# Bucket attention and a GELU feed-forward on one core: the softmax division of batch 0 moves from the probabilities to the product with V

## The chip, the cores and the metric

The kernel runs on one core of one Trainium2 chip. The metric is the device time of one execution in microseconds (us). Three executions of the kernel before took 891.5, 893.44 and 896.03 us, with a median of 893.44. The profile shown here is of one execution of 893.21 us; its span, from the first to the last instruction, is 891.4 us, and 1.8 us lie around it.

Engines are named as the profile names them: PE is TensorE (PEld its weight loads), DVE is VectorE, ACT is ScalarE, POOL is GpSimd, SP is SyncE, which issues most of the transfers.

## The reference

Attention over 4 batches of 8 heads with 768 positions and 64 channels, in which a query sees only the keys of its own hash bucket (6 sign bits of a projection), and then a feed-forward layer 512 → 2048 → 512 with an exact GELU over the 3072 rows:

```python
mask = q_bucket[:, :, :, None] == k_bucket[:, :, None, :]
scores = scale * np.matmul(q, k.transpose(0, 1, 3, 2))
scores = np.where(mask, scores, -1000000000.0)
scores = scores - np.max(scores, axis=-1, keepdims=True)
attn = np.exp(scores)
attn = attn / (np.sum(attn, axis=-1, keepdims=True) + 1e-09)
attn_out = np.matmul(attn, v).astype(np.float32)
...
h = x @ w_in
g = 0.5 * h * (1.0 + erf(h * inv_sqrt2))
return (g @ w_out).astype(np.float32)
```

## The kernel before, in words

**Attention.** The work is cut into units: one head and 128 queries against all 768 keys, 48 units in a batch, 192 in all. A unit (`unit`, L938) computes its scores on PE into a PSUM buffer `s` (there are two), takes their largest per row on DVE (L960), makes a scale and a shift from it in two tiny operations (L965, L438 or L434, buffer `rows`), and takes the exponential on ACT (L974), which also delivers the sum of each row. The exponentials stand in a buffer `p` (or, in a slot that is lent later, in `wraw`). A tiny operation adds 1e-9 to the sum (`safe`, L979) and a reciprocal on DVE (L983) makes the factor r.

Batch 0 then goes the float32 way (`whole_turn`, L1024; the setting `WHOLE` says for which pairs of heads, and it is all four pairs in both passes over batch 0): `divide` multiplies the 128x768 exponentials by r, on ACT, DVE or POOL (POOL in two halves of 384); PE transposes them in six blocks of 128x128, three to a PSUM bank `hp` (L1033); ACT or DVE copies each bank into `pt`. Batches 1 to 3 go another way: r is applied while the exponentials are split into two float16 parts `hl`, which a DMA transposes.

For two heads and a chunk of 256 queries, `values` (L1062) multiplies V by the transposed probabilities on PE into one `hp` bank, the two heads in the two halves of the partitions (L1077 in batch 0, L1086 later). Then `high` on ACT (L1107) writes the upper float16 part of the chunk's input x to the feed-forward, and `low` on DVE (L1114) the rest; both read the PSUM bank, and in batch 0 both multiply by V's scale `s_v`. Batch 0 has 4 pairs of heads and 3 chunks, so 12 such products.

**Feed-forward.** For each chunk of 256 rows there are two groups of eight blocks of the 2048 hidden columns. Each group multiplies x by `Win` (L1302), is taken out of PSUM with a scale by ACT (L1312), goes through GELU on ACT (L1340), is split into two float16 parts `g`, and is multiplied by `Wout` (L1384). The weights come as raw 64-bit numbers, are decoded by DVE (L725 to L735) and split by ACT, DVE and POOL during the first 200 us.

**The order.** All of it is a list of steps with needs, buffers and a sort key. `Plan.order` (L120) runs the list through a model of the engines: whenever an engine is free it takes the ready step with the smallest key, and steps that may go to several engines go to whichever takes them first. The instructions are then issued in the order of the starts that the model found. The keys come from the table `PAR`. Each engine executes its own list strictly in order.

**Blanks.** `add_blank` (L389) adds 64 steps of four products of zeros on PE (L393) which need nothing and have the last key of all, so the plan puts one wherever its PE would have nothing else to do, until the 64 are used. They hold one `hp` bank for their time.

```python
        step = add("PE", 0.22, products, 5000.0, [], takes="hp")
        free(step, [step])
```

Of the kernel before, what the change touches and what calls it, by code (L numbers as in the profile page):

```python
# [10 lines left out]
F32 = mybir.dt.float32  # L11
# [22 lines left out]
BLANKS = 64  # L34
# [3 lines left out]
    VB=67.25, GU_DVE=142.88, GU_Pool=372.81, SH_DVE=-85.93, SH_ACT=493.57, SH_Pool=68.35, SF_DVE=-887.75,  # L38
    SF_ACT=162.31, SF_Pool=108.68, SU=-62.77, NM_DVE=132.71, NM_ACT=-36.16, NM_Pool=115.43, NM_SP=44.22,
    NL_DVE=-21.95, NL_Pool=-504.75, XP_ACT=-123.39, XP_DVE=180.18, NK_DVE=-90.24, NK_ACT=-257.23, NK_Pool=-55.95,  # L40
    Z=-107.86, VS0=65.79, H0=-112.84, HL=-846.73, VS=-934.16, G2=389.39, HQ=129.83, VQ=-373.79, in0=-133.17,
    out0=545.05, in1=-218.36, out1=37.81, in2=194.95, out2=21.39, in3=465.04, out3=52.59, H1=3.14, H2=-183.97,
    H3=-155.9, H4=131.48, H5=-603.75, H6=-1004.23, H7=-195.76, MEV=266.52, MGE=696.78, MSP=15.46, V0=-120.7,
    QK0=-118.82, QK1=-287.83, QK2=-180.25, MX0=-320.05, MX1=-49.19, MX2=-219.29, EX0=-612.78, EX1=-167.36,
    EX2=70.44, NR0=-89.58, NR1=33.83, NR2=-17.38, HI0=-561.14, HI1=248.83, HI2=340.6, LO0=106.64, LO1=-1263.75,
    LO2=-161.71, PV0=99.03, PV1=115.36, PV2=-77.27, TR0=-1005.23, TR1=-480.94, TR2=45.98, V1=105.26, V2=-194.1,
    Sin0=149.2, Sin1=64.71, Sin2=7.41, Sin3=246.53, Sout0=-231.58, Sout1=-272.11, Sout2=-372.59, Sout3=194.04,
    Lin=-157, Pin=341.2, Qin=1120.37, Cin=100.83, Min=-140.12, Lout=-105.73, Pout=458.37, Qout=-2863.3,
    Cout=-238.38, Mout=162.39, G0=-122.8, G1=-209.72, G3=488.78, G4=20.46, G5=-83.65, G6=-236.82, G7=27.83,
    DUP0=78.15, DUP1=-85.93, DUP2=-123.07, LOW0=-97.07, LOW1=-66.78, LOW2=18.58, PRJ0=-51.38, PRJ1=841.88,  # L50
    PRJ2=-212.69, MSK0=-114.42, MSK1=426.71, MSK2=228.3, DI_ACT=138.03, DI_DVE=-27.21, DI_Pool=-60.85,
    WS_ACT=419.32, WS_DVE=65.06, WS_Pool=-21.69, WH_ACT=-803.88, WH_DVE=7.52, WH_Pool=-245.54, WL_ACT=-154.68,
    WL_DVE=-7.58, WL_Pool=72.47, VH_ACT=-163.46, VH_DVE=-112.9, VH_Pool=63.2, RND_ACT=86.42, RND_DVE=222.34,
    RND_Pool=221.18, HI_ACT=230.76, HI_DVE=-182.55, HI_Pool=-59.39, DG_ACT=-153.24, DG_DVE=84.64, DG_Pool=151.66,
    EV_ACT=296.59, EV_DVE=1365.55, EV_Pool=34.42, GH_ACT=-144.99, GH_DVE=2.32, GH_Pool=-76.31, NS0=220.81,
    NS1=-94.09, NS2=63.07,
# [7 lines left out]
class Step:  # L64
    def __init__(self, seq, engine, cost, emit, key, needs, takes, table, port, act):
# [5 lines left out]
        self.takes, self.table, self.port, self.act = takes, table, port, act  # L71
        self.needs = [n for n in needs if n is not None]
        self.slot = None
        self.frees = []
        self.start = self.end = None


class Plan:
# [19 lines left out]
    WINDOW = 3.413  # L98

# [4 lines left out]
    def add(self, engine, cost, emit, key, needs=(), takes=None, table=None, port=False, act=1.0):  # L104
        s = Step(len(self.steps), engine, cost, emit, key, needs, takes, table, port, act)
        self.steps.append(s)
        return s
# [12 lines left out]
    def order(self):  # L120
# [33 lines left out]
        while events:  # L154
# [4 lines left out]
            for e in batch:  # L159
# [11 lines left out]
                for u in users.get(e, ()):  # L171
                    left[u] -= 1
                    for w in u.ways:
                        hop = self.SAME.get(w, 0.05) if w == e.engine else self.HOP[e.engine] + self.INTO.get(w, 0.0)
                        at[u, w] = max(at.get((u, w), 0.0), now + hop)
                        heapq.heappush(events, (at[u, w], -1, None))
                    if not left[u]:
                        enlist(u)
            for engine, pool in ready.items():
                if free_at[engine] > now or not pool:  # L180
                    continue
                best = None
                for s in pool:
# [12 lines left out]
                if best is None:  # L196
                    continue
# [20 lines left out]
                if engine == "PE":  # L218

                    while window < int(now / self.WINDOW):  # L220
                        share = busy.get(window, 0.0) / self.WINDOW
                        warm = share > (0.35 if warm else 0.8)
# [19 lines left out]
                count += 1  # L242
                heapq.heappush(events, (free_at[engine], -1, None))
                heapq.heappush(events, (s.end, s.seq, s))
        assert count == len(self.steps), [
            (list(s.ways), s.key, s.takes) for s in self.steps if s.start is None
        ][:10]
        self.time = max(s.end for s in self.steps)
        return sorted(self.steps, key=lambda s: (s.start, s.seq))
# [3 lines left out]
def tile_bucket_attention_moe(  # L253
# [64 lines left out]
    rows = const.tile([P, NT, 6], F32, tag="rows", name="rows")  # L318
    tiny = const.tile([P, 4 * NSC + 2 * B, 4], F32, tag="tiny", name="tiny")
# [58 lines left out]
    hs = const.tile([P, B * H + 3, 8], F32, tag="hs", name="hs")  # L378
# [10 lines left out]
    def add_blank():  # L389
# [5 lines left out]
        step = add("PE", 0.22, products, 5000.0, [], takes="hp")  # L395
# [50 lines left out]
    def affine_on(name, n, pointer=False, psum=False):  # L446

        more = 0.11 if name in ("MV", "MSK", "RND") else 0.0
        return {
            e: (affine_cost(e, n, pointer) + more, PAR[f"{name}_{e}"]) for e in ("ACT", "DVE", "Pool")  # L450
        }

    def subtract_on(name, n):
        return {e: (subtract_cost(e, n), PAR[f"{name}_{e}"]) for e in ("DVE", "Pool")}
# [1021 lines left out]
```

## Time and profile before

| | |
|---|---|
| median of three executions | 893.44 us |
| profiled execution, its span | 893.21 us, 891.4 us |
| mean granted TensorE clock | 0.996 of full |
| PE instructions | 6893 matmuls |
| units of attention, whole way and float16 way | 48 and 144 |
| exponentials on `p` before 210 us | 49 |

A line of the list of groups reads: kernel line, engine, operation, tile written <- tiles read, shapes, count, then busy time in us and the mean ns of one, then the idle time of the engine just before such instructions and what ended most of it. A line of a stretch gives, for each engine, its busy us and in brackets its number of instructions, then the granted TensorE clock as a part of full speed (1.00 is 2.4 GHz, 0.50 is 1.2 GHz; values between are stretches with both), then DMA. A matmul's time is that from its start to its result, and neighbours overlap; so the time that a series takes is read from the timeline, where instructions in a row are merged, and not from count times mean. L438 is the multiply-and-add on DVE or POOL, L434 the one on ACT, whatever uses them.

### The profile page before, as it was taken

The page shows a single profiled execution, that of the slowest core. Times are in us where ns is not written, and L with a number is a line of the kernel's source. Part 1 is how long each engine was busy: PE and PEld are TensorE (multiplying, and loading weights), DVE is VectorE, ACT ScalarE, POOL GpSimd, SP SyncE. Part 2 cuts the span into 40 slices and gives each one's busy share as a digit, 9 for nine tenths or more (in the row PEclk, how much of TensorE's full clock was granted, in tenths as well). Part 3 has the DMA queues.
Part 4 walks back from the last instruction along what each step waited for, and adds up shares of the span by engine and source line. Part 5 has one row for each costly group of instructions (what it writes and reads, how often), then busy time and mean ns, then how long its engine had stood idle before and what let it go on. Part 6 is the DMA issues. An engine that isn't in the chain of part 4 may idle for free. (4 is left out here: it accounts for less than half of the span.)

```text
span 891.4 us, 18270 instructions
## 1 busy us (share of the span) xinstructions
PE 860.6 (97%) x6893; PEld 574.3 (64%) x6893; DVE 675.9 (76%) x1441; ACT 648.6 (73%) x1090; POOL 419.4 (47%) x551
## 2 busy tenths in 40 slices
PE   8999899989999999999999999999999999999998
PEld 5666557655756657667657657657657667676663
DVE  4998999888997999898999898898887851212122
ACT  3788889998897898898998797887877643232221
POOL 2485759686656566655764666455523300000000
PEclk9999999999999999999999999999999999999999
DMA  9952454215687898778879786957766740000000
GB/s 252 258 174 89 117 151 136 72 46 119 145 174 156 167 205 180 150 152 160 170 159 199 155 183 139 179 102 151 135 107 123 132 96 1 24 2 24 1 24 24
DMA packets 282392, 112.15 MB, mean 126 GB/s; under 512 B 228800, under 2 KB 269888, under 8 KB 282304
## 3 DMA queue, kind: packets, MB, share of 16 engines
q1 hardware_dynamic: 282000, 110.98, 57.6%
q8 instruction: 54, 0.88, 0.4%
q14 instruction: 34, 0.28, 0.1%
q10 hardware_dynamic: 304, 0.00, 0.0%
HBM read 43.13 MB, written 6.29 MB: 55 GB/s over the span
## 5 line engine op out<-in xcount | busy, mean ns | idle before, releaser
L1302 PE MATMUL hp<-x,Win 128*128 128x256 f16 x2304 | 265.5, 272 | 1.6 <-DVE x L1114 1.2
L1384 PE MATMUL hp<-Wout,g 128*128 128x512 f16 x1152 | 261.5, 379 | 0.0
L1302 PEld LDWEIGHTS <-Win 128*128 128x128 f16 x2304 | 224.4, 98 | 39.9 <-issue 4.4
L1384 PEld LDWEIGHTS <-g 128*128 128x128 f16 x1152 | 109.9, 98 | 126.3 <-issue 4.4
L960 DVE TENSOR_REDUCE rows<-s 128x1 f32<-128x768 f32 x192 | 179.2, 948 | 8.3 <-PE s L957 5.2
L974 ACT ACTIVATE p<-s,rows 128x768 f32<-128x768 f32 x142 | 140.2, 988 | 19.9 <-POOL rows L438 7.9
L1312 ACT ACTIVATE h<-hp,ffs 128x512 f32<-128x512 f32 x96 | 65.5, 683 | 98.8 <-PE hp L1302 98.2
L956 PE MATMUL s<-Q 88*128 88x384 f16 x304 | 99.4, 327 | 8.2 <-ACT p L974 5.3
L957 PE MATMUL s<-K 128*128 128x384 f16 x304 | 99.2, 326 | 0.0
L438 DVE TENSOR_SCALAR g<-h,ffs 128x512 f16<-128x512 f32 x30 | 15.2, 507 | 108.1 <-ACT h L1340 77.9
L1086 PE MATMUL hp<-pt,vhl 128*64 128x256 f16 x1296 | 77.1, 274 | 0.5 <-DVE o L1414 0.2
L989 DVE SCALAR_TENSOR_TENSOR hl<-p,rows,hl 128x768 f16<-128x768 f32 x66 | 74.1, 1126 | 3.6 <-POOL hl L438 2.0
L1354 DVE SCALAR_TENSOR_TENSOR g<-h,ffs,g 128x512 f16<-128x512 f32 x96 | 73.4, 787 | 2.7 <-ACT g L434 0.6
L1086 PEld LDWEIGHTS <-vhl 128*64 128x64 f16 x1296 | 68.9, 110 | 10.1 <-issue 9.3
L965 POOL TENSOR_SCALAR rows<-rows,hs 128x1 f32<-128x1 f32 x67 | 46.0, 687 | 61.8 <-DVE rows L960 58.1
L438 POOL TENSOR_SCALAR rows<-rows 128x1 f32<-128x1 f32 x109 | 44.2, 406 | 58.3 <-ACT p L974 35.5
L459 POOL TENSOR_TENSOR K<-raw,Q 64x768 f16<-64x768 f32 x40 | 67.7, 1694 | 3.3
L974 ACT ACTIVATE wraw<-s,rows 128x768 f32<-128x768 f32 x50 | 49.4, 988 | 9.4 <-POOL rows L438 3.9
L438 POOL TENSOR_SCALAR raw<-raw,hs 64x768 f32<-64x768 f32 x41 | 46.7, 1139 | 17.9 <-ACT Q L434 8.6
L957 PEld LDWEIGHTS <-K 128*128 128x128 f16 x304 | 29.8, 98 | 30.6 <-issue 13.9
L438 DVE TENSOR_SCALAR rows<-rows 128x1 f32<-128x1 f32 x163 | 28.3, 180 | 26.8 <-ACT p L974 19.6
L438 POOL TENSOR_SCALAR Q<-sign 24x384 f16<-24x384 f16 (+1 forms) x52 | 32.5, 626 | 33.4 <-ACT sign L674 18.5
(169 smaller groups left out, 1366.5 us busy)
## 6 DMA issues: line engine op xcount, KB each, us to landing
raw<-qk SPq DMA_DIRECT2D x27, 384.0 KB, 3.8
vraw<-v SPq DMA_DIRECT2D x24, 384.0 KB, 4.1
wraw<-w_in SPq DMA_DIRECT2D x16, 512.0 KB, 6.1
wraw<-w_out SPq DMA_DIRECT2D x16, 512.0 KB, 4.1
out<-o SPq DMA_DIRECT2D x11, 512.0 KB, 2.9
K<-Q SPq DMA_DIRECT2D x31, 96.0 KB, 2.4
Q<-Q SPq DMA_DIRECT2D x17, 96.0 KB, 2.7
pt<-hl SPq DMA_TRANSPOSE x97, 4.1
```

What stands on the lines that cost most here:

```text
L438: on.tensor_scalar(out=o, in0=x, scalar1=scale, scalar2=bias, op0=ALU.mult, op1=ALU.add)
L459: on.tensor_tensor(out=o, in0=x, in1=y, op=ALU.subtract)
L956: nc.tensor.matmul(to, aq[kk, qs], ak[kk, n], start=True, stop=False)
L957: nc.tensor.matmul(to, bq[:, qs], bk[:, n], start=False, stop=True)
L960: nc.vector.tensor_reduce(out=nm, in_=both(sp), axis=AX.XY, op=ALU.max, negate=True)
L974: nc.scalar.activation(out=buf(ex).rearrange("p (b k) -> p b k", b=2), in_=both(sp), func=AF.Exp, scale=sc, bias=nb, accum_out=ssum,)
L989: nc.vector.scalar_tensor_tensor(out=buf(hi)[:, 1], in0=buf(ex), scalar=r, in1=buf(hi)[:, 0], op0=ALU.mult, op1=ALU.subtract,)
L1086: nc.tensor.matmul(pv[j * D : (j + 1) * D], buf(vh)[:, tv, kt, j * D : (j + 1) * D], buf(holds[j][0])[:, tp * KT + kt, :nt], start=kt == 0 ...
L1302: nc.tensor.matmul(buf(pair[0])[:, j * ch[1] : (j + 1) * ch[1]], win_hl[:, f0 // WB1, tw, pr, f0 % WB1 : f0 % WB1 + P], x[:, tx, pr, : ch[1]],
L1312: nc.scalar.activation(out=values_of()[:, 2 * fp : 2 * fp + 2, :nt], in_=buf(pair[0])[:, : 2 * nt].rearrange("p (j k) -> p j k", j=2), fun ...
L1354: nc.vector.scalar_tensor_tensor(out=gt[:, 1, s2, :nt], in0=h[:, s2, :nt], scalar=sg, in1=gt[:, 0, s2, :nt], op0=ALU.mult, op1=ALU.subtract,)
L1384: nc.tensor.matmul(buf(banks[u]).rearrange("p (c f) -> p c f", c=NWB), gt[:, tg, f, u * P : (u + 1) * P], wout_hl[:, :, tw, ft], start=ft ...
```

## The change

Four edits.

1. In batch 0 the exponentials are transposed undivided. `unit` writes the row sums of both heads of a pair and a chunk into a tile `sums`. A new function `shares` adds 1e-9 to the four columns of a chunk, takes their reciprocals, and lets PE spread them: for each block of 128 queries and each head, one float32 product of a column, repeated 64 times as weights, with the identity, so that a `hp` bank holds each query's factor in the column of that query, in the 64 partitions of its head. ACT or DVE copies that bank into a buffer of the ring `hl`. In `values`, a DVE operation `weigh` multiplies the product with V by `s_v` and by the factors and writes the result over the factors in that buffer; `upper` (ACT, DVE or POOL) and `lower` (DVE or POOL) make x's two parts from there.
2. There may be up to 128 blanks. The plan puts one only while its own count of PE's recent busy share is at most 0.7, and it ends when all other steps are placed.
3. Some costs and one threshold in the plan's model are changed (the weights' split on POOL is 0.35 to 0.5 us dearer; the model's clock falls at a share of 0.45 instead of 0.35).
4. The table `PAR` has new values throughout, and with them and the above the order of all instructions on all engines is new, their DMAs included.

```diff
-BLANKS = 64
+BLANKS = 128
...
+    FILL = 0.7
+    FALLS = 0.45
...
+                if engine == "PE":
+                    w = int(now / self.WINDOW)
+                    share = busy.get(w, 0.0) / self.WINDOW
+                    share += busy.get(w - 1, 0.0) / self.WINDOW * (w + 1 - now / self.WINDOW)
+                    full = share > self.FILL
...
+                    if s.spare and full:
+                        continue
...
-        step = add("PE", 0.22, products, 5000.0, [], takes="hp")
+        step = add("PE", 0.22, products, 5000.0, [], takes="hp", spare=True)
...
+        if whole:
+            ssum = into
...
+        if whole:
+            return sp, whole_turn(ex, place, cl, t), ex
...
-        if whole:
-            return sp, whole_turn(ex, nr, r, place, cl, t)
...
-        def divide():
-            affine(dg.engine, buf(ex), buf(ex), r, most=512)
...
+    def shares(n, nt, exs, key):
+
+        share = sums[:, n, : nt // P].rearrange("p u j -> p (u j)")
+
+        def sure():
+            affine(sf.engine, share, share, 1.0, 1e-9)
+
+        def norm():
+            nc.vector.reciprocal(out=share, in_=share)
+
+        def spread():
+            for u in range(nt // P):
+                for j in range(2):
+                    nc.tensor.matmul(
+                        buf(rt)[j * D : (j + 1) * D, words(u)],
+                        sums[:, n, u, j : j + 1].broadcast_to([P, D]), ident32, start=True, stop=True,
+                    )
+
+        def copy():
+            affine(rc.engine, wide(rc)[:, :nt], buf(rt)[:, :nt])
...
+            def weigh():
+                nc.vector.scalar_tensor_tensor(
+                    out=wide(share)[:, :nt], in0=buf(parts[0])[:, :nt], scalar=s_v[:, b : b + 1],
+                    in1=wide(share)[:, :nt], op0=ALU.mult, op1=ALU.mult,
+                )
+
+            def upper():
+                if (b, ch) != first_ch:
+                    go_late()
+                affine(hi.engine, buf(xt[b, ch])[:, 0, pr, :nt], wide(share)[:, :nt])
+
+            def lower():
+                x = buf(xt[b, ch])
+                subtract(lo.engine, x[:, 1, pr, :nt], wide(share)[:, :nt], x[:, 0, pr, :nt])
```

## Rows read from the trace of the kernel before

**Rows 1.** The page's first part: busy us, share of the span and number of instructions of each engine over the whole span.

```profile
PE 860.6 (97%) x6893; PEld 574.3 (64%) x6893; DVE 675.9 (76%) x1441; ACT 648.6 (73%) x1090; POOL 419.4 (47%) x551
```

**Rows 2.** Busy time of each engine in five stretches of the span, with the granted clock.

```profile
0.00:25.00 25.00, 21.30 (x235) 15.98 (x236) 13.66 (x36) 10.41 (x19) 6.98 (x26) 0.93 0.94 262
25.00:75.00 50.00, 48.18 (x352) 31.40 (x350) 45.55 (x114) 41.34 (x82) 35.51 (x56) 0.97 0.67 184
75.00:205.00 130.00, 118.29 (x918) 80.12 (x917) 118.98 (x300) 118.28 (x213) 90.87 (x132) 1.00 0.36 102
205.00:715.00 510.00, 500.35 (x4196) 333.71 (x4194) 453.15 (x922) 427.50 (x718) 285.68 (x337) 1.00 0.78 154
715.00:891.40 176.40, 172.51 (x1208) 113.11 (x1202) 44.61 (x73) 51.10 (x61) 0.31 (x1) 1.00 0.09 25
```

**Rows 3.** The timeline of all engines from 886 us to the end.

```profile
885.62 1.89 PE L1384 MATMUL hp<-Wout,g 128*128 128x512 f16 x8
...
887.55 0.69 DVE L1414 TENSOR_TENSOR o<-hp,ffs 128x512 f32<-128x512 f32 x1 [4.49 <-PE hp L1384]
888.27 0.34 SPq L1427 DMA_DIRECT2D out<-o  x1
```

**Rows 4.** The blanks alone (L393), PE and PEld busy in four stretches.

```profile
0.00:25.00 25.00, 13.80 (x174) 12.95 (x175) 0.93 0.94 262
25.00:75.00 50.00, 5.27 (x74) 4.50 (x71) 0.97 0.67 184
75.00:205.00 130.00, 0.83 (x12) 0.76 (x12) 1.00 0.36 102
205.00:715.00 510.00, 0.00 (x0) 0.00 (x0) 1.00 0.78 154
```

**Rows 5.** Who waited for whom from 75 to 205 us: total us, times, longest.

```profile
PEld s L954 <- ACT p L974: 5.7, 9, 1.6
PE s L954 <- ACT p L974: 3.4, 5, 1.5
...
PE hp L1033 <- ACT pt L434: 1.6, 5, 0.4
```

**Rows 6.** ACT's groups of the first 210 us that the change touches, with the copies into `pt`.

```profile
L434 ACT ACTIVATE p<-p,rows 128x768 f32<-128x768 f32 x30 | 27.8, 934 | 5.6 <-DVE rows L983 4.9 <-DVE rows L965 0.4
L434 ACT ACTIVATE pt<-hp 128x384 f32<-128x384 f32 x60 | 27.2, 485 | 3.4 <-PE hp L1033 3.2
...
L434 ACT ACTIVATE rows<-rows 128x1 f32<-128x1 f32 x24 | 5.7, 243 | 2.6 <-DVE rows L965 1.3 <-POOL rows L965 0.9
L1107 ACT ACTIVATE x<-hp,s_v 128x256 f16<-128x256 f32 x12 | 5.6, 467 | 0.8 <-PE hp L1077 0.5
...
L434 ACT ACTIVATE wraw<-wraw,rows 128x768 f32<-128x768 f32 x2 | 1.9, 928 | 0.0
```

**Rows 7.** The same of DVE.

```profile
L438 DVE TENSOR_SCALAR pt<-hp 128x384 f32<-128x384 f32 x36 | 19.5, 548 | 2.9 <-PE hp L1033 2.8
L983 DVE RECIPROCAL rows<-rows 128x1 f32<-128x1 f32 x52 | 8.1, 157 | 2.4 <-POOL rows L438 1.2 <-ACT rows L434 0.9
L438 DVE TENSOR_SCALAR rows<-rows 128x1 f32<-128x1 f32 x48 | 8.0, 176 | 3.5 <-ACT p L974 2.9 <-ACT wraw L974 0.2
L1114 DVE SCALAR_TENSOR_TENSOR x<-hp,s_v,x 128x256 f16<-128x256 f32 x12 | 5.7, 476 | 0.5 <-ACT x L1107 0.5
L438 DVE TENSOR_SCALAR p<-p,rows 128x768 f32<-128x768 f32 x5 | 3.3, 655 | 0.2
```

**Rows 8.** The same of POOL, with its subtractions of 128x256.

```profile
L459 POOL TENSOR_TENSOR Wout<-o,Wout 128x256 f16<-128x256 f32 x24 | 16.4, 713 | 0.1
L438 POOL TENSOR_SCALAR p<-p,rows 128x384 f32<-128x384 f32 x22 | 15.7, 723 | 8.5 <-DVE rows L983 6.2 <-DVE hs L569 1.6 <-DVE tiny L406 0.6
L438 POOL TENSOR_SCALAR rows<-rows 128x1 f32<-128x1 f32 x32 | 14.0, 437 | 14.7 <-ACT p L974 11.1 <-DVE rows L965 1.2 <-DVE hs L569 0.6
```

**Rows 9.** Groups of the whole span whose shapes are nearest to the new operations.

```profile
L1107 ACT ACTIVATE x<-hp 128x256 f16<-128x256 f32 x36 | 13.3, 372 | 10.3 <-PE hp L1086 10.2
...
L459 DVE TENSOR_TENSOR Wout<-o,Wout 128x1024 f16<-128x1024 f32 x2 | 2.5, 1252 | 0.0
...
L438 DVE TENSOR_SCALAR diag<-ident,tiny 128x128 bf16<-128x128 bf16 x3 | 0.7, 245 | 0.0
```

**Rows 10.** PE's timeline from 126 us: start, time of the whole run, number of instructions.

```profile
127.63 1.48 PE L1033 MATMUL hp<-ident,p 128*128 128x128 f32 x12
...
131.17 2.81 PE L1077 MATMUL hp<-pt,vhl 128*64 128x256 f32 x24
...
136.67 1.12 PE L748 MATMUL hp<-Wout 128*64 128x64 bf16 x32
```

**Rows 11.** The weight loads of the products with V (L1077) and of the transposes before 210 us.

```profile
L1033 PEld LDWEIGHTS hp<-ident,p 128*128 128x128 f32 x276 | 31.1, 142 | 16.3 <-issue 4.4 <-ACT pt L434 2.0 <-ACT p L434 1.9
...
L1077 PEld LDWEIGHTS hp<-pt,vhl 128*64 128x64 f32 x192 | 13.3, 137 | 10.2 <-DVE pt L438 1.6 <-ACT pt L434 1.3 <-DVE rows L983 0.5
```

**Rows 12.** PE's timeline from 62 us, around the lower clock.

```profile
65.54 0.70 PE L668 MATMUL hp<-rest,hash 128*32 128x384 f16 x7 [1.24 <-DMA rest<-x]
66.17 1.54 PE L1033 MATMUL hp<-ident,p 128*128 128x128 f32 x6
67.51 2.26 PE L954 MATMUL s<-K,Q 76*128 76x384 f32 x4
...
73.33 1.46 PE L954 MATMUL s<-K,Q 76*128 76x384 f32 x4
```

**Rows 13.** Busy times and granted clock in the stretch that holds the lower clock.

```profile
66.00:70.00 4.00, 4.00 (x20) 2.84 (x18) 1.76 (x3) 3.25 (x7) 4.00 (x7) 0.61 0.47 146
```

**Rows 14.** PE's waits in the whole span.

```profile
PE s L956 <- ACT p L974: 5.3, 13, 1.3
...
PE s L956 <- ACT wraw L974: 2.2, 2, 1.5
```

**Rows 15.** PE's timeline from 20 us, the longest run of blanks.

```profile
22.02 3.30 PE L393 MATMUL hp<-blank 128*128 128x128 bf16 x56
```

**Rows 16.** The instructions of batch 0's products with V: count, duration in ns (least, median, most), start of the first and of the last.

```profile
L1077 PE MATMUL hp<-pt,vhl x192: 379/379/430, 104.1 to 207.4; 128*64 128x256 f32 x192
...
L1077 PE MATMUL hp<-pt,v_first x96: 379/379/431, 39.6 to 86.7; 128*64 128x256 f32 x96
```

More of the change, by code (lines that the diff above doesn't have):

```diff
@@ L64, with __init__ @@
 class Step:
-    def __init__(self, seq, engine, cost, emit, key, needs, takes, table, port, act):
+    def __init__(self, seq, engine, cost, emit, key, needs, takes, table, port, act, spare=False):
         many = isinstance(engine, dict)
@@ L153, in order @@
         count, serial = 0, -1
-        while events:
+        total, again = sum(not s.spare for s in self.steps), 0.0
+        while events and count < total:
             now, _, ended = heapq.heappop(events)
@@ L196, in order @@
                 if best is None:
+                    if full and again <= now:
+                        again = now + 0.3
+                        heapq.heappush(events, (again, -1, None))
                     continue
@@ L241, in order @@
                         heapq.heappush(events, (port_at, -1, None))
-                count += 1
+                count += not s.spare
                 heapq.heappush(events, (free_at[engine], -1, None))
                 heapq.heappush(events, (s.end, s.seq, s))
-        assert count == len(self.steps), [
+        assert count == total, [
             (list(s.ways), s.key, s.takes) for s in self.steps if s.start is None
         ][:10]
-        self.time = max(s.end for s in self.steps)
-        return sorted(self.steps, key=lambda s: (s.start, s.seq))
+        done = [s for s in self.steps if s.start is not None]
+        self.time = max(s.end for s in done)
+        return sorted(done, key=lambda s: (s.start, s.seq))
 @with_exitstack
@@ L936, in head_plain, with unit @@
         return masks, None
-    def unit(t, i, qs, cl, whole, made, place, back):
+    def unit(t, i, qs, cl, whole, made, place, back, into):
         st = rows[:, t % NT]
         nm, sc, nb, ssum, si, r = (st[:, k : k + 1] for k in range(6))
+        if whole:
+            ssum = into
         def both(step):
@@ L1046, in whole_turn @@
             step.append(
[L1047 removed]
+                add("PE", 0.12 * (k1 - k0), lambda k0=k0, k1=k1, step=step: product(k0, k1, step), t + PAR[f"LO{cl}"], [ex], takes="hp")
             )
@@ L1060, in whole_turn, with wide, values @@
         return copies
-    def values(b, pr, ch, whole, vhl, turns, holds, key):
+    def wide(step):
+        return buf(step).rearrange("p t k -> p (t k)").bitcast(F32)
+    def shares(n, nt, exs, key):
[13 more added lines that the diff above has]
+            affine(rc.engine, wide(rc)[:, :nt], buf(rt)[:, :nt])
+        on = {"DVE": (0.09, PAR["SF_DVE"]), "ACT": (0.23, PAR["SF_ACT"]), "Pool": (0.3, PAR["SF_Pool"])}
+        sf = add(on, 0, sure, key + PAR["RN"], exs)
+        nr = add("DVE", 0.08, norm, key + PAR["RN"], [sf])
+        rt = add("PE", 0.24 * nt / P, spread, key + PAR["RT"], [nr], takes="hp", table="half")
+        rc = add(
+            {e: (c, PAR[f"RC_{e}"]) for e, c in (("ACT", 0.31), ("DVE", 0.34))}, 0, copy, key + PAR["RT"], [rt], takes="hl"
+        )
+        free(rt, [rc])
+        return rc
+    def values(b, pr, ch, whole, vhl, turns, holds, key, share):
         vh, vl = vhl
@@ L1213, in tile_bucket_attention_moe @@
                 if pos % 2:
+                    share = shares(pr * NTH + ch[0] // TC, ch[1], exs[ch], t + PAR[f"PV{cl}"]) if whole else None
                     mms.append(
```

114 lines of the change are left out of this document (56 added, 58 removed).

## The prediction

> **What bounds the kernel now.** I read the page's first part, then the stretches, then the end of the timeline, then the waits. PE is busy 97% of the span [rows 1], and the end is PE's: the last product runs until DVE's drain at 887.55 and its store [rows 3]. So the time is the sum of PE's work plus whatever time PE idles or spends on blanks before, and I look for where that is. In 205 to 715 us PE is busy 500.35 of 510 us, 98.1%, with no blank; from 715 on it only streams [rows 2, 4]. The waste is early. In 0 to 25 us 13.8 us of PE's 21.3 are blanks, while the first loads and hashes come in; the change removes no load and no hash from that. In 25 to 205 us, 180 us, PE is busy 48.18 + 118.29 = 166.5 us, of which 5.27 + 0.83 = 6.1 are blanks [rows 2, 4]; so 19.6 us of this stretch bring nothing. What it waits for there is mostly a score buffer that ACT's exponential has not yet freed [rows 5], and ACT is busy 41.3 + 118.3 = 159.6 us of the 180, DVE 45.6 + 119.0 = 164.5, POOL 126.4 [rows 2]. In 75 to 205 us both ACT and DVE stand at 91%: this stretch is bound by the pair. Batch 0's float32 products with V start from 39.6 to 207.4 us [rows 16], so the work that is changed lies there.
>
> **What the change takes away.** 48 divisions of 128x768: 30 + 2 on ACT (27.8 + 1.9 = 29.7 us), 5 on DVE (3.3), 11 on POOL in 22 halves (15.7) [rows 6 to 8]. Of 48 additions of 1e-9 and 48 reciprocals, 12 each remain. The reciprocals save DVE 36 x 0.157 = 5.7 us [rows 7]. The additions are among 24 + 48 + 32 = 104 tiny operations on ACT, DVE and POOL; taking out 36 in these shares saves 8 x 0.243 = 2.0, 17 x 0.176 = 2.9 and 11 x 0.437 = 4.8 us [rows 6 to 8]. The old `high` and `low` of x go: 5.6 us on ACT, 5.7 on DVE [rows 6, 7]. In sum ACT 37.3, DVE 17.6, POOL 20.5: 75.4 us.
>
> **What it adds beside PE.** Twelve times four operations of 128x256. The copy of the factors is nearest to the unscaled read of PSUM, 0.372 us on ACT [rows 9]. `weigh` has the shape of the old `low`, 0.476 us [rows 7]. `upper` lies between 0.245 (a quarter-size multiply on DVE [rows 9]) and 0.723 (128x384 on POOL [rows 8]); I take 0.37, ACT's. `lower` lies between a quarter of the 1.252 us of 128x1024 on DVE, 0.31 [rows 9], and POOL's 0.713 [rows 8]; I take 0.42, nearer to DVE's. That makes 12 x 1.64 = 20 us, with ends 12 x 1.40 = 17 and 12 x 2.28 = 27. The net relief is 55 us, with ends 48 and 58, and on ACT and DVE alone 54.9 - 20 = 35 us when POOL takes none. Copies into `pt` may go to either (60 and 36 of them, 0.485 and 0.548 us [rows 6, 7]), so a relief of ACT reaches DVE too: ten copies moved give DVE 5.5 us.
>
> **What it adds on PE.** 48 float32 products with 128 columns, two heads side by side. A product with V is 12 of 256 columns, and its 24 records take 2.81 us [rows 10], so a side-by-side pair of 256 columns takes 0.47 us and one of 128 columns half, 0.234. 24 pairs make 5.6 us. From below: if 96 short records go as the 64-column products of the weights do, 1.12 / 32 = 0.035 us each [rows 10], 3.4 us. From above: as the transposes do, 1.48 / 12 = 0.123 us each [rows 10], 11.8 us. I take 5.6, from the row of the same kind and dtype.
>
> What the Trainium skill says on the loads speaks against this ("TensorE: Matmul & The Clock Gate", Part 3: Packing small matmuls): a weight load overlaps running products only if it goes to other rows of the array, and both heads' factors use all 128 rows. By it each of 96 loads would stand open; the trace disagrees, for 24 such loads of 0.137 us [rows 11] would alone be 3.3 us and the whole product took 2.81 [rows 10].
>
> **From both to the time.** In 25 to 205 us ACT and DVE carry 324 of 360 us, 90%. With 35 less, at the same density, the stretch would need 289 / 0.90 / 2 = 161 us: 19 less. But PE must do its share as well: 166.5 - 6.1 + 5.6 = 166.0 us, and at the density of the later stretch, 98.1%, that takes 169.2 us. So PE becomes the bound of this stretch, and the gain stops at 10.8 us (13 with the lower price of the spreading, 4.5 with the higher). I take 9: not all of the first heads' stretch can reach the later density, since float32 heads arrive singly. After 205 us nothing of the work changes, and each us won there is won at the end. 893.2 - 9 = 884.2 for this execution, and with the median 0.2 above it 884.4.
>
> **What I cost at nothing.** The new chain (exponentials, addition, reciprocal, spreading, copy, `weigh`, `upper`, `lower`) delays x by some 1.5 us against the old pair. It hides behind the other units' scores and transposes; without that cover it is 12 x 1.5 = 18 us, but only PE's products with `Win` wait for x, and for the first chunk they come long after. The spreading waits for DVE's reciprocal with transposes and scores queued behind it on PE; a transpose no longer waits for a reciprocal and a division, so this queue has gained more slack than it loses. The factors' buffer comes from a ring that batch 0 doesn't use. More blanks: PE is charged only where the plan saw it idle; a run of 56 products takes 3.30 us [rows 15], 0.059 each, so 64 more steps of four cost at most 15 us, if each stood in front of ready work, and nothing if none does; I take nothing, since the plan gives them the last key. They can win back the lower clock at 66 to 70 us (0.61 [rows 13], after a wait of 1.24 us): there four products took 2.26 instead of 1.46 us and six transposes 1.54 against half of 1.48, so 1.6 us [rows 10, 12]. The dearer weight splits and the threshold change only the plan. The new order moves every DMA on SP's queue and every step on POOL's; DMA is 36% busy in 75 to 205 us [rows 2], so I give that nothing, within bounds of -5 to +15 us that stand for the order as a whole: from below half of the 9.65 us that PE idles in 205 to 715, from above twice the idle share there less what the early stretch gives.
>
> **The rivals.**
> - *The relief isn't passed on.* The early units are paced by a chain (scores, largest, exponential, freed buffer) and not by load. For it: PE's waits are for two score buffers [rows 5]. Against it: that exponential is late because ACT is at 91%. Then the spreading takes idle time and the time stays: 892, from 889 to 896.
> - *The order loses in the full stretch* (slower). In 205 to 715 us ACT is 84% and DVE 89% busy, and PE's few waits there are for freed score buffers, 5.3 + 2.2 us in the whole span [rows 14]. If the new order starts each of the 140 later units' exponentials so late that PE waits 0.13 us more, that is 18 us, and 893 - 9 + 18 = 902 (897 to 910). It decides from 9 / 140 = 0.064 us a unit on. Against it: nothing there has more work than before.
> - *The order gains there too.* Half of the 9.65 us of idle time goes, and the early gain is near its upper end: 893 - 13 - 4 = 876 (870 to 879).
> - *The weight loads stand open.* 96 x 0.137 = 13.2 us more on PE: 166.5 - 6.1 + 18.8 = 179.2, or 182.7 at 98.1%, so 896. It is the rule of the Trainium skill named above; [rows 10, 11] speak against it.
>
> **How the numbers follow.** A gain of 4.5 to 14 us, 884.4: 0.48 (its own range 879 to 889). Not passed on: 0.21. Lost in the full stretch: 0.17. Gains twice: 0.09. Open loads: 0.05. 0.5% is 4.5 us, about what a measurement of this kernel can tell from no change: under 889 is faster, over 898 slower. Faster: 0.47 + 0.09 + 0.03 = 0.59; within: 0.01 + 0.17 + 0.04 = 0.22; slower: 0.17 + 0.01 + 0.01 = 0.19. The range 873 to 900 leaves out the far half of the slower case and a third of the best.
>
> **What would show it.** Right: in the first 210 us ACT has some 33 us less to do, no group `p<-p,rows` of 128x768 float32 is left, 96 records of 64 columns stand on PE and take about 5.6 us, the last batch-0 product with V (now starting at 207.4 us [rows 16]) comes some 9 us earlier relative to the feed-forward work done, and PE's idle time from 205 to 715 us stays near 10 us. Wrong: ACT is relieved and PE's waits for score buffers remain; or PE's idle time after 205 us has grown by more than 9 us; or a spreading takes over 0.6 us.

## The result: slower by half a percent, and the profile after

The changed kernel takes 898.34 us (median of 20 executions, 892.61 to 901.91) beside 893.58 us of the kernel before (20 executions, 889.18 to 896.03): a ratio of 1.0052, 95% interval 1.0035 to 1.007. The forecast was 884.4, a ratio of about 0.99. The time lies inside the range, but on the wrong side of 1. By the medians the miss is 13.9 us; the experiments below give 8.1 of them to TensorE's clock and 5.9 to a relief that brought little.

The profiled execution happened to be the fastest of the 20 (892.61 us, granted clock 0.994). An unchanged copy run again (`ctl_after`) took 899.88 us, and its profiled execution, 899.19 us with a span of 897.4, lies near the median; I read that one. Its page's first part, beside [rows 1]:

```profile
PE 872.1 (97%) x6869; PEld 581.7 (65%) x6869; DVE 681.9 (76%) x1387; ACT 615.1 (69%) x1064; POOL 407.7 (45%) x507
```

Over the whole span ACT lost 33.5 us of work and POOL 11.7. DVE, which was to lose 17.6 us less its share of the new work, gained 6.0, and PE gained 11.5. The same five stretches as in [rows 2]; the columns are PE, PEld, DVE, ACT and POOL busy, then the granted clock:

```profile
0.00:25.00 25.00, 21.59 (x121) 11.60 (x122) 13.78 (x37) 11.57 (x21) 6.70 (x22) 0.64 0.94 248
25.00:75.00 50.00, 48.06 (x287) 30.09 (x286) 41.78 (x87) 28.69 (x63) 21.33 (x33) 0.84 0.58 175
75.00:205.00 130.00, 122.72 (x1011) 86.42 (x1010) 115.09 (x264) 106.60 (x205) 80.19 (x107) 0.96 0.38 108
205.00:715.00 510.00, 500.99 (x4206) 336.25 (x4205) 460.96 (x921) 413.58 (x707) 295.75 (x342) 1.00 0.77 152
```

Two things are to be seen. The full stretch from 205 us on is as it was: PE idles 9.0 us there against 9.65. And the clock column has fallen, 0.64 and 0.84 where it was 0.93 and 0.97. Cut more finely:

```profile
0.00:7.00 7.00, 3.59 (x38) 3.41 (x42) 0.93 (x8) 0.00 (x0) 2.59 (x16) 1.00 0.66 152
7.00:40.00 33.00, 32.28 (x164) 16.83 (x157) 23.78 (x48) 17.78 (x33) 8.09 (x14) 0.50 1.03 294
...
93.00:106.00 13.00, 12.01 (x39) 8.20 (x40) 7.60 (x16) 6.96 (x16) 6.36 (x7) 0.61 0.33 94
```

From 7 to 40 us, and for most of the time from 93 to 106 us, PE runs at 0.50, its level of 1.2 GHz. The kernel before had 2.4 GHz but for some 3 us between 11 and 15 us and a part of the 4 us of [rows 13]. It too fell over a wait of 2.08 us; but there 36 blanks followed, 0.106 us each instead of the 0.059 of [rows 15], and behind them the hash products take 0.51 us again and eight score records 2.85 us:

```profile
11.00 0.19 PE L560 MATMUL hp<-tops,twin 128*128 128x1 bf16 x2 [2.08 <-DVE tops L603]
11.05 3.80 PE L393 MATMUL hp<-blank 128*128 128x128 bf16 x36
14.78 0.51 PE L907 MATMUL hp<-Q,hash 64*32 64x384 f32 x1
...
18.46 2.85 PE L954 MATMUL s<-K,Q 76*128 76x384 f32 x8
```

PE's timeline of `ctl_after` (start, length of the run, number of instructions, and the wait ahead of it) shows what that means:

```profile
6.68 0.19 PE L531 MATMUL hp<-offs,shift 128*128 128x1 bf16 x2 [2.43 <-DVE offs L527]
6.80 0.51 PE L923 MATMUL hp<-Q,hash 64*32 64x384 f32 x1
...
9.33 0.85 PE L923 MATMUL hp<-Q,hash 64*32 64x384 f32 x1
...
10.77 2.93 PE L972 MATMUL s<-K,Q 76*128 76x384 f32 x4
...
36.28 3.59 PE L408 MATMUL hp<-blank 128*128 128x128 bf16 x32
...
90.41 0.50 PE L1047 MATMUL hp<-ident,p 128*128 128x128 f32 x3
93.94 1.14 PE L1047 MATMUL hp<-ident,p 128*128 128x128 f32 x6 [3.03 <-DVE tiny L786]
...
97.76 2.77 PE L972 MATMUL s<-K,Q 76*128 76x384 f32 x4
```

Four records of a score step take 2.77 to 2.93 us instead of the 1.46 of [rows 12], a hash product 0.85 instead of 0.51. Each fall follows a wait, one of 2.43 us that ends at 6.68 us and one of 3.03 us that ends at 93.94 us. The blanks alone, to be laid beside [rows 4]:

```profile
0.00:25.00 25.00, 5.35 (x50) 5.09 (x51) 0.64 0.94 248
25.00:75.00 50.00, 5.91 (x56) 5.13 (x54) 0.84 0.58 175
```

The kernel before had 174 blank products in its first 25 us, the changed one has 50. `BLANKS` was doubled, but steps that the new rule (only while PE's recent share is under `FILL`) never finds a place for are not issued: of 128 steps, 34 are left with 136 products, against 64 with 256.

In `ctl_after` the groups of the whole span that answer to [rows 6 to 9] and to the spreading are

```profile
L453 DVE TENSOR_SCALAR pt<-hp 128x384 f32<-128x384 f32 x28 | 15.2, 549 | 1.2 <-PE hp L1047 1.2
L1167 DVE SCALAR_TENSOR_TENSOR hl<-hp,s_v,hl 128x256 f32<-128x256 f32 x12 | 5.8, 482 | 1.9 <-PE hp L1124 1.7
L475 DVE TENSOR_TENSOR Wout<-o,Wout 128x1024 f16<-128x1024 f32 x4 | 5.5, 1371 | 0.1
L475 DVE TENSOR_TENSOR Win<-o,Win 128x1024 f16<-128x1024 f32 x2 | 3.3, 1632 | 0.0
...
L475 POOL TENSOR_TENSOR Wout<-o,Wout 128x256 f16<-128x256 f32 x16 | 11.2, 730 | 0.9 <-ACT Wout L449 0.8
...
L449 ACT ACTIVATE pt<-hp 128x384 f32<-128x384 f32 x68 | 31.2, 490 | 21.7 <-PE hp L1047 21.0
...
L1091 PE MATMUL hp<-ident,sums 128*64 128x128 f32 x96 | 7.8, 283 | 0.7 <-ACT pt L449 0.4 <-DVE rows L983 0.3
```

No group `p<-p,rows` of 128x768 float32 is left. Eight copies into `pt` went from DVE to ACT. Four weight differences went the other way, from POOL to DVE: DVE now does six in 8.8 us where it did two in 2.5 [rows 9], and POOL issues 16 quarters for `Wout` where it issued 24 [rows 8], and 24 for `Win` where it issued 32.

### The profile page after: what moved, and what is told of

Its sections match the earlier page's. It is cut to its first block, busy times and chain, and to the rows that moved or that the text cites. A ratio compares the mean times of both kernels' runs of the same rounds, so it can differ in the third digit from the quotient of the medians.

```text
span 890.8 us, 18120 instructions
## 1 busy us (share of the span) xinstructions
PE 865.2 (97%) x6869; PEld 577.6 (65%) x6869; DVE 681.3 (76%) x1387; ACT 615.3 (69%) x1064; POOL 411.9 (46%) x507
## 4 chain that ended last, share of the span: by engine, by line
PE 56%; DVE 18%; ACT 9%; DMA 9%; issue 4%; POOL 4%; SPq 0%; ACTq 0%; POOLq 0%; DVEq 0%
PE hp L1445 19%; PE hp L1363 18%; PE hp L1133 6%; DVE rows L978 4%; PE s L972 3%; PE s L974 3%; PE s L975 3%; DMA pt<-hl 3%; DVE hl L1007 3%; ACT p L992 2%; PE hp L1124 2%; DMA vraw<-v 2%; DVE g L1415 2%; DMA pt<-wraw 2%; PE hp L1047 1%
## 5 line engine op out<-in xcount | busy, mean ns | idle before, releaser
L992 ACT ACTIVATE p<-s,rows 128x768 f32<-128x768 f32 x144 | 142.3, 989 | 27.3 <-DVE hl L1007 8.5
L453 DVE TENSOR_SCALAR g<-h,ffs 128x512 f16<-128x512 f32 x24 | 12.4, 516 | 109.6 <-ACT h L1401 78.9
L1007 DVE SCALAR_TENSOR_TENSOR hl<-p,rows,hl 128x768 f16<-128x768 f32 x66 | 70.7, 1073 | 8.0 <-POOL hl L453 5.4
L983 POOL TENSOR_SCALAR rows<-rows,hs 128x1 f32<-128x1 f32 x58 | 37.3, 644 | 58.8 <-DVE rows L978 53.5
L475 POOL TENSOR_TENSOR K<-raw,Q 64x768 f16<-64x768 f32 x37 | 61.9, 1674 | 3.1
L992 ACT ACTIVATE wraw<-s,rows 128x768 f32<-128x768 f32 x48 | 47.4, 987 | 9.9 <-POOL rows L453 5.4
L453 POOL TENSOR_SCALAR hl<-p,rows 128x768 f16<-128x768 f32 x29 | 33.9, 1168 | 33.0 <-DMA pt<-hl 16.6
L972 PE MATMUL s<-K,Q 76*128 76x384 f32 x112 | 47.7, 560 | 1.3 <-ACT p L992 1.0
L453 POOL TENSOR_SCALAR raw<-raw,hs 64x768 f32<-64x768 f32 x39 | 43.3, 1110 | 9.4 <-ACT Q L449 6.0
```

The source lines that it names most:

```text
L453: on.tensor_scalar(out=o, in0=x, scalar1=scale, scalar2=bias, op0=ALU.mult, op1=ALU.add)
L972: nc.tensor.matmul(to, q[:, qs], k[:, n], start=True, stop=True)
L992: nc.scalar.activation(out=buf(ex).rearrange("p (b k) -> p b k", b=2), in_=both(sp), func=AF.Exp, scale=sc, bias=nb, accum_out=ssum,)
L1007: nc.vector.scalar_tensor_tensor(out=buf(hi)[:, 1], in0=buf(ex), scalar=r, in1=buf(hi)[:, 0], op0=ALU.mult, op1=ALU.subtract,)
```

## The experiments

A new plan moves every step, so all runs keep the order of one of the two kernels and edit only what is issued. Each is compared with the kernel before, timed beside it on the same chip. CLOCK is the theory that the lost blanks and the lower clock are the loss.

**The same kernel again**, unchanged.

> The changed kernel once more, unaltered, for a second profile. Theory CLOCK (the changed kernel emits 34 blanks instead of 64, 44 instead of 174 of their products in the first 25 us, and TensorE therefore runs at 1.2 GHz in stretches that differ from execution to execution): 896 to 900 us, with a profile in which other or more stretches than 88 to 98 us stand at the lower clock, and the hash products of the first 24 us again take 0.84 us instead of 0.5. Theory ORDER (the new order of the instructions loses, whatever the clock): the same time, but the lost time appears as waits of PE with the clock at full speed.

Measured: 899.88 us (895.0 to 902.9, 8 executions) beside 892.53, ratio 1.007 (1.0038 to 1.0102). The result stands.

**Fewer blanks in the old order.** The blank steps 11 to 43 of the kernel before are issued empty:

```diff
-        add_blank()
+        add_blank(0 if 11 <= n < 44 else 4)
```

> The kernel before with its order kept; of its blanks in the first 25 us only the first 11 emit products (44, as in the changed kernel). CLOCK: PE stays at 1.2 GHz until past 20 us and the time rises by 4 to 8 us, to 898 to 902. LOADS: no change within 1.5 us.

Measured: 900.8 us (897.28 to 905.48), ratio 1.0084 (1.0055 to 1.0113). PE's timeline in its profile:

```profile
17.57 5.49 PE L954 MATMUL s<-K,Q 76*128 76x384 f32 x8
22.99 0.85 PE L907 MATMUL hp<-Q,hash 64*32 64x384 f32 x1
```

The kernel before took 2.85 us for eight such score records. So the blanks that the change no longer issues are worth 8 us in the old order, with nothing else changed. That is CLOCK, as expected, and more than the whole loss; LOADS falls. The 8 us are not the first 25 us alone: this profile has a second fall, 0.65 from 96 to 106 us and 0.77 from 106 to 120 us, where the kernel before has 1.00.

**Only a warm start.** In the changed kernel the first eight blank steps have six products; in the profile of this run the wait that ends at 6.6 us is 1.14 us long, instead of 2.43.

```diff
-        add_blank()
+        add_blank(6 if n < 8 else 4)
```

> The changed kernel with its order kept; only the first eight blanks have 6 products instead of 4 each, so that they fill the 2.03 us in which PE waits for its first input at 4.6 to 6.6 us. CLOCK: PE is at 2.4 GHz from about 7 us on, the hash products and the first scores take half of what they took, and since PE is busy without a pause there, the time falls by 6 to 8 us, to 890 to 892. A rival, LOADS (the first 25 us are paced by the loads, the DMA engines being busy throughout, so the clock there is free): no change within 1.5 us.

Measured: 899.92 us, ratio 1.0077 (1.0048 to 1.0105): missed. The hash products ran in 0.51 us until 14.2 us; then, after float32 work with waits of 0.63 and 0.66 us, the clock fell all the same and stayed down until 39 us. A warm start doesn't hold by itself.

**Relief alone, in the old order.** The kernel before, leaving out batch 0's additions, reciprocals and divisions; the factor 1/32 in the copies stands for them.

```diff
-            affine(dg.engine, buf(ex), buf(ex), r, most=512)
+            pass
```

> The kernel before with its order kept, without batch 0's 48 divisions, additions and reciprocals: that part of the softmax is left out (the copies into pt multiply by 1/32 to keep the sums in range). This gives the relief of ACT, DVE and POOL that the prediction priced, without the spreading and without a new order. Theory RELIEF (the early stretch is bound by ACT and DVE): 5 to 12 us less, 881 to 888. Rival NOT PASSED ON (PE and chains bind it): within 2 us of before.

Measured: 889.91 us, ratio 0.9956 (0.9929 to 0.9983), 2.6 us less at the median; missed by both expectations, between them. ACT from 75 to 205 us fell from 118.28 to 97.64 us and PE still waited for score buffers:

```profile
PE s L954 <- ACT p L974: 2.5, 5, 0.9
PE hp L560 <- DVE pt L438: 1.4, 1, 1.4
PE hp L1079 <- DVE pt L438: 1.2, 1, 1.2
```

Taking 20 us from ACT took 0.9 us from the 3.4 of that wait [rows 5].

**The clock held in the new order.** Blank products are issued ahead of chosen hash, score and transposing steps of the first 40 us, into the PSUM bank that the step overwrites anyway, and during the wait at 84 to 91 us into unused columns of the bank before:

```diff
+            warm("project", buf(pp)[:, :P])
...
+            if nth["product"] == 34:
+                for k in range(40):
+                    nc.tensor.matmul(turned[0][:, 3 * P :], blank, blank, start=True, stop=True)
```

> The changed kernel with its order as it is and 132 more blank products of 128 columns on TensorE: 48, 40 and 28 of them as a prefix in the PSUM bank of a hash, score or transposing step of the first 40 us, 16 in the first eight blank steps (6 products instead of 4), and 40 into the unused columns of a bank during the wait of 2.6 us at 84 us (172 in sum). Nothing of the result changes. CLOCK (the loss is TensorE at 1.2 GHz early on): hash products last 0.48 to 0.51 us throughout the first 45 us, the granted clock stays near 1.00 from 75 to 110 us, and the time falls by 5 to 12 us against the changed kernel, to 886 to 893, ratio to the kernel before 0.993 to 1.000. ORDER or SPREADING (the loss lies elsewhere): the clock is repaired and the time stays at 896 to 900.

> As after_warm, without the 40 products in the wait at 84 us: only the first 40 us are filled. CLOCK: the hash products of the first 45 us at 0.48 to 0.51 us, the lower clock again for some 10 us after the wait at 84 to 91 us, and the time between after_warm and the changed kernel, 2 to 5 us above after_warm. If the second stretch of lower clock costs nothing (TensorE isn't the bound there), the two times agree within 1 us.

The counts in the first text are off: it was 68, 36 and 28 products as a prefix, 16 at the start and 40 in the wait, 188 in sum. Measured: `after_warm` 891.24 us (889.19 to 900.37), ratio 0.9981 (0.9946 to 1.0017). Seven of its ten executions had a granted clock of 0.999 or more and took 889.19 to 891.63 us; the other three, at 0.991 and 0.992, took 895.11 to 900.37. `after_warm_a`, without the 40, took 899.39 us, ratio 1.0038 (0.9998 to 1.0079), 8 us above `after_warm` where 2 to 5 were expected: missed. So the 40 products in the one wait are worth 8 us at the median. The first 40 us must hold too: the profiled execution of `after_warm`, one of the slow three with 900.37 us, fell behind a wait of 1.28 us that ends at 26.07 us, stood at 0.54 from 25 to 40 us, and kept 1.00 from 60 us on. In the profile of `after_warm_a` the first 40 us held (no hash product over 0.51 us) and PE stood at 0.50 from 90 to 96 us. So in these runs either fall alone costs about as much as both; why they don't add up was not shown. The next run puts 32 more blanks at the first place:

```diff
+            n_blank[0] += 1
-            for k in range(4):
+            for k in range(EXTRA["blank"].get(n_blank[0], count)):
```

> after_warm with 32 more blank products in four of the changed kernel's own blank steps at 24 to 27 us (16, 16, 8 and 8 instead of 4 each), where the profiled execution of after_warm fell to the lower clock behind a wait of 1.3 us. Nothing of the result changes. CLOCK: the executions stay at a granted clock of 1.00 nearly all, so their spread shrinks to some 889 to 893 and the median is 890 to 892, 7 to 9 us under the changed kernel and 2 to 4 under the kernel before. If the fall at 25 us has another cause than that wait, a third of the executions is still at 895 to 900.

Measured: 890.26 us (888.71 to 892.34, 12 executions, all at 0.999 or 1.000), ratio 0.9957 (0.9931 to 0.9984). Its stretches:

```profile
0.00:25.00 25.00, 22.38 (x257) 17.05 (x258) 13.97 (x37) 11.87 (x22) 6.75 (x23) 1.00 0.95 245
25.00:75.00 50.00, 48.19 (x368) 31.54 (x366) 45.90 (x96) 31.99 (x71) 21.76 (x34) 1.00 0.63 193
75.00:205.00 130.00, 124.58 (x1087) 88.80 (x1086) 118.77 (x279) 111.79 (x210) 87.94 (x113) 1.00 0.36 104
```

and the wait filled:

```profile
86.17 0.49 PE L1074 MATMUL hp<-ident,p 128*128 128x128 f32 x3
86.50 2.40 PE L1070 MATMUL hp<-blank 128*128 128x128 bf16 x40
88.73 0.82 PE L1074 MATMUL hp<-ident,p 128*128 128x128 f32 x6
```

CLOCK holds: with the order untouched and 220 more products of zeros, the changed kernel is 8 us faster than it was, and the spread of its executions shrinks from 9 us to 3.6. In its profile no hash product of the first 45 us takes more than 0.62 us.

**The old order at the same clock.**

```diff
+            warm("total", buf(pm)[:, :P])
             for k in range(n):
                 nc.tensor.matmul(buf(pm)[:, k : k + 1], twin[:, k], top, start=True, stop=True)
```

> The kernel before with its order as it is and 116 blank products where its own profile and that of before_nodiv fell to the lower clock: 36 and 16 ahead of two scale steps at 11 and 99 us, 16 and 12 ahead of two hash steps at 64 and 97 us, 12 ahead of a score step at 99.5 us, 12 and 12 ahead of two transposing steps at 66 and 97.5 us. Nothing of the result changes. It puts the two orders beside each other at the same clock. If the change's relief is worth something beside the clock, this stays 4 us or more above after_warm2, at 893 to 895. If the clock is all that told the two kernels apart and the relief and the spreading cancel, it comes to 889 to 892, level with after_warm2 within 2 us.

Measured: 894.02 us, ratio 0.9997 (0.997 to 1.0025). Level with before, and no proof that the change is worth 4 us: its 116 blanks stood partly ahead of ready work. Without them, 11 of the 110 executions of the kernel before that were timed beside these runs had a clock of 0.998 or more by themselves; they took 889.87 to 892.46 us, median 890.85. That is a rough mark, for these executions are picked by a column that can read too high early on (see the last section). By it the change at a held clock gives 0.6 us (890.26), no more than nothing, and the relief alone gave 4 (`before_nodiv`: four executions at 0.998 or more, median 886.7).

**The price of the spreading.** Its products twice in the changed kernel, and none (two blanks in the place of eight) with the clock held:

```diff
-            for u in range(nt // P):
+            for u in 2 * [*range(nt // P)]:
```

> The changed kernel with each of its 96 spreading products issued twice (the second to the same place with the same value), 0.6 us more on TensorE for each of the 12 steps, 7.1 us in sum. If TensorE is the bound of the early stretch, the time grows by 5 to 8 us, to 904 to 907, and the spreading of the change itself is paid in full. If it stands in TensorE's waits (the relief isn't passed on and there is idle time), it grows by less than 3 us.

```diff
-                for j in range(2):
...
+                nc.tensor.matmul(buf(rt)[:, words(u)], blank, blank, start=True, stop=True)
```

> after_warm2 with the spreading left out: in each of its 12 steps two blank products of 128 columns stand for the eight products with the sums, so batch 0's rows of x become zero; all else is as it was. That takes 0.59 - 0.12 = 0.47 us from TensorE in each step, 5.6 us in sum. If TensorE sets the pace of the early stretch once its clock is held, the time falls by 4 to 6 us, to 884 to 886. If the spreading stands in TensorE's waits, it falls by less than 2 us.

Measured: doubled 901.61 us, ratio 1.0073 (1.0036 to 1.0111) where `ctl_after` has 1.007, so 0.3 us more by the ratios and 1.7 by the medians, for 7.1 us of PE; left out 889.98 us beside the 890.26 of `after_warm2`, ratios 0.9953 and 0.9957, for 5.6 us less. The spreading stands in PE's waits. The stretches without it, to be laid beside those of `after_warm2`:

```profile
25.00:75.00 50.00, 47.23 (x353) 31.27 (x350) 46.25 (x98) 31.95 (x71) 21.93 (x34) 1.00 0.62 192
75.00:205.00 130.00, 121.19 (x1035) 86.06 (x1034) 117.53 (x279) 112.22 (x211) 88.45 (x113) 1.00 0.36 104
```

PE's busy time fell by 4.4 us and the others' moved by less than 1 us: idle time took its place. PE doesn't set the pace here.

**The division put back in the new order.**

```diff
+                affine(on, buf(ex), buf(ex), 1.0, most=512)
             for k in range(k0, k1):
```

> The changed kernel with a multiplication by 1.0 of 128x768 float32 put back in front of each of the 48 pairs of transposes (32 on ACT, 11 on POOL, 5 on DVE, as the divisions were), in the new order. Nothing of the result changes. If the relief of the change is passed on in the new order, the time grows by 8 to 13 us; if it isn't, by less than 4 us; the kernel before without its divisions gained only 3 to 4 us in its own order.

Measured: 934.92 us, ratio 1.0466, far above either expectation. In its first 240 us PE waited 35.5 us for the multiplied `p` (21.9 on ACT's, 11.0 on POOL's, 2.6 on DVE's): the new plan puts transposes right behind the exponential, and the division now stands between them. This prices a late input in a tight order, not the relief, and I draw nothing else from it.

**Which engine sets the pace, then?** Still with the clock held:

```diff
-                    box[2].engine, dst[:, 1], buf(box[0]).rearrange("p (c f) -> p c f", c=n), dst[:, 0],
+                    "Pool", dst[:, 1], buf(box[0]).rearrange("p (c f) -> p c f", c=n), dst[:, 0],
```

> after_warm2 with the six weight differences that stand on DVE (6 of 16; 5.5 + 3.2 = 8.7 us) issued on POOL instead, at the same place of the order, as 24 quarters of some 0.73 us. Nothing of the result changes. If DVE paces the early stretch, because the change took nothing from it (178.2 us of its work in the first 205 us before, 178.6 in after_warm2), the time falls by 3 to 8 us, to 882 to 887. If DVE isn't what paces it, or what waits for POOL is late instead, it stays at 889 to 892 or above.

```diff
+                for _ in range(2 if box[2].engine == "DVE" else 1):
```

> after_warm2 with the same six weight differences issued twice on DVE (the same result written again), 8.7 us more on DVE. If DVE paces the early stretch, the time grows by 6 to 9 us, to 896 to 899. If DVE has room there, it grows by less than 3 us.

```diff
+                for _ in range(2 if box[1].engine == "ACT" else 1):
```

> after_warm2 with the ten weight copies on ACT (5.3 + 5.1 = 10.4 us) issued twice, 10.4 us more on ACT, which has 10 to 15 us more idle time in the early stretch than before the change. If DVE alone paces the stretch, the time grows by less than 3 us. If ACT does (the pair of ACT and DVE, as the prediction has it), it grows by 5 us or more.

Measured: 898.36, 905.61 and 906.27 us, beside 893.07; ratios 1.0049 (1.0017 to 1.0081), 1.0123 and 1.0129. All three are slower, the one with less work on DVE too. Part is the clock again; PE's timeline of `dve_less`:

```profile
119.55 1.56 PE L994 MATMUL s<-K,Q 76*128 76x384 f32 x4 [1.80 <-ACT p L1014]
120.94 0.22 PE L509 MATMUL hp<-diag,ones 128*128 128x128 bf16 x1
121.00 1.25 PE L1074 MATMUL hp<-ident,p 128*128 128x128 f32 x6
122.05 2.77 PE L994 MATMUL s<-K,Q 76*128 76x384 f32 x4
```

A wait of 0.4 us in `after_warm2` is 1.80 us here, and a new fall follows it, at a place where no blanks were put. In all three profiles the clock column reads 0.92 from 75 to 205 us, where `after_warm2` has 1.00, so a part of each growth is the clock and not the moved work. Where the column reads 0.998 or more, five executions of `dve_less` took 895.0 us at the median, 4.7 above `after_warm2`, and the only one of `dve_more` 901.89, 11.6 above; `act_more` has none. `dve_less` settles less than it was meant to: the differences took 8.7 us on DVE and take some 15 us on POOL, and PE's wait for POOL's `diag`, 0.6 us in `after_warm2`, is now its longest single wait between 25 and 205 us:

```profile
PE hp L509 <- POOL diag L472: 2.6, 1, 2.6
```

So it doesn't tell whether DVE paces the stretch; that DVE alone does is spoken against by `act_more`, which grew as much as `dve_more`. As far as these runs go, work added to DVE is paid in full (one execution), work added to ACT at least in part, and work taken from PE, or handed from DVE to POOL, isn't given back.

**A version that beats both.** `after_warm2` with 48 of its blanks taken out again:

```diff
-    "project": {1: 16, 2: 12, 3: 16, 4: 12, 6: 12},
-    "scores": {0: 8, 1: 12, 2: 8, 3: 8},
-    "product": {0: 16, 2: 12},
+    "project": {1: 16, 2: 8, 3: 12, 4: 8},
+    "scores": {0: 8, 1: 8},
+    "product": {0: 12, 2: 12},
```

> after_warm2 with 48 fewer added blank products: none ahead of the two score steps at 28 and 30 us and of the hash step at 31 us, which stood behind other blanks in front of ready work, and 4 fewer in each of five other places. Nothing of the result changes. If the blanks that are left hold the clock, the time falls by up to 48 x 0.06 = 2.9 us, to 887.5 to 890; if they don't, a part of the executions is at 895 to 900.

Measured: 889.05 us (885.07 to 891.56), ratio 0.9937 (0.9911 to 0.9963): 0.6% under the kernel before and 1% under the changed one. That doesn't take a clock held throughout: its profiled execution, 888.53 us, stood at 0.50 from 22 to 28 us, until 32 blanks had run.

## Why the prediction was wrong, step by step

**The step that failed first** is "More blanks: PE is charged only where the plan saw it idle ... I take nothing", with its sequel that more blanks "can win back the lower clock". I read the doubled count and not the rule beside it. The rule leaves fewer blanks, not more, and the clock was worth not 1.6 us on the good side but 8 on the bad one: `before_fewblanks` (8.3 us more) shows it without the change, `after_warm2` (8.1 us less) undoes it within the change. The sum started from a kernel whose 13.8 us of early blanks I had put down as waste [rows 4]; they were what kept the float32 work of the first 40 us at 2.4 GHz.

**The second** is "From both to the time". It took 35 us from ACT and DVE between 25 and 205 us and turned them into time at an equal density. Neither came out. Of the 35 us, `after_warm2` shows 15.8 on ACT (159.6 [rows 2] to 143.8) and none on DVE (164.5 to 164.7). The terms for DVE were right one by one (no divisions, fewer reciprocals, 5.8 us of `weigh` beside 5.7 forecast), but "the dearer weight splits ... change only the plan" was taken at nothing, and it moved 6.3 us of differences to DVE; with the weights' other steps DVE got 8 us and ACT 4 that POOL had done. And the density was no bound: `before_nodiv` took 25.2 us from ACT and 3.2 from DVE in that stretch without any of the change's costs, and 2.6 us came of it, 4 by the executions with a held clock. In the forecast PE idled 3.2 us of what was left of the stretch from 25 to 205 us and did no blanks; in `after_warm2` it idles 7.2 of the 180 us and does 11 us of blanks, those of the plan and the added ones. With 7.1 us of spreading that is more than the 19.6 us which I had counted as free.

**The spreading** was forecast at 5.6 us and measures 12 x 0.59 = 7.1 on PE (from the start of a step's eight records to the next step, 0.59 instead of 0.47); inside its bounds of 3.4 and 11.8, and worth nothing in the time. A step's own run reads 0.61 to 0.66 us, over the 0.6 us that I had named as a sign of being wrong; that mark stood too near to tell anything. The rival of the open weight loads is refuted: eight records with loads of 0.136 us take 0.66 us, less than eight loads in a row.

**The rivals.** "The order loses in the full stretch" had the right sign and the wrong place: 9.0 us of idle time there. That the time lies in the range at all is owed to this rival, so it is luck. "The relief isn't passed on" is what is left at a held clock, though not for its reason, since PE's waits for float32 score buffers between 25 and 205 us did shrink, from 3.6 us to 1.3 in `ctl_after` and 2.0 in `after_warm2`. Of the marks that I named, the missing group and the idle time after 205 us came as forecast. The relief of ACT in the first 210 us did not: some 33 us were named, and it is 20.7 in `ctl_after` (172.6 to 151.9) and 12.0 in `after_warm2`; the last of batch 0's products with V starts at 211.7 us in `ctl_after` and at 204.7 in the fastest execution, against 207.4 [rows 16].

**What stays open** is what paces the early stretch at a held clock. It isn't PE, and `act_more` speaks against DVE's load alone; that it is the fixed order itself, in which each engine waits in its list for one late input after another, fits the runs but was not shown.

## What to carry to other kernels

Blanks are not waste until a run without them says so: before a share of "useless" work is booked as free, look at what clock the work around it would have. A change of a planner's rule is read by what it issues (count the instructions in each stretch), not by the constant that grew. And in an order written out ahead, little of what is taken away comes back by itself (2.6 us for 28 us of ACT and DVE, nothing for 5.6 us of PE), while added work was paid; whether an order made anew would give it back was not shown.

## What the runs showed of the hardware

PE can be busy without a pause and stay at the lower clock. In `ctl_after` it is busy 16.00 of the 16 us from 8 to 24 us, mostly with float32 hash, score and transposing products, and is granted 0.50 throughout:

```profile
8.00:24.00 16.00, 16.00 (x72) 7.16 (x73) 11.88 (x28) 9.81 (x20) 3.72 (x5) 0.50 1.06 284
```

It rose during the score step right behind a run of 32 bfloat16 blanks (36.28 to 39.87 us), and in the kernel before it rose at the end of the 36 blanks from 11.05 us on. Once at 2.4 GHz, the same float32 products kept it: in `after_warm2`, behind the 40 blanks, the score steps and transposes from 88.73 to 97 us all run at 2.4 GHz, four score records in 1.46 to 1.56 us. The Trainium skill ("TensorE: Matmul & The Clock Gate", Part 1: The HAM clock gate) says that the clock is low after idle time and that activity releases the throttle. The first agrees with the waits of 2.43 and 3.03 us here; as to the second, these 16 us without a pause on the profile's PE row did not release it.

The clock column can read 1.00 where it isn't: in the profile of the changed kernel's fastest execution it stands at 1.00 from 7 to 25 us, and the durations there up to 24 us are those of 1.2 GHz:

```profile
9.58 0.85 PE L923 MATMUL hp<-Q,hash 64*32 64x384 f32 x1
...
11.02 2.93 PE L972 MATMUL s<-K,Q 76*128 76x384 f32 x4
```

The same holds for `before_fewblanks`, whose column reads 1.00 from 7 to 25 us over hash products of 0.85 us. So early on the level is to be read from the length of a known product, 0.51 or 0.85 us, before it is read from the column, and a mean clock of 0.998 for a whole execution doesn't prove a held clock in its first 25 us.
